# Attention with an expert layer behind it: four more of the 24 attention steps turned by VectorE, and the routing begun half a pair sooner

## Chip, cores and metric

The kernel runs on one core of one Trainium2 chip. The metric is the device time of one execution in microseconds (us); lower is better. Several runs are taken and their median is given.

## What is computed

Two layers, one behind the other, in float32.

```python
# attention: B, H, S, D = 4, 8, 768, 64, in blocks of 64 rows, with a decay lam per head
for each block:
    intra = ((q k^T) * Dmask) v
    out   = intra + (q * lam_pow) kv_state
    kv_state = lam**64 * kv_state + (k * rev_pow)^T v
x = out as (B, S, 512)
# expert layer: 8 experts, 512 -> 1024 -> 512
logits = x @ w_gate; keep = sigmoid(x @ w_local) >= 0.5
e[b, s] = e[b, s-1] if keep[b, s] and s > 0 else argmax(logits[b, s])
out[b, s] = softmax(logits[b, s])[e] * (relu(x[b, s] @ w1[e]) @ w2[e])
```

Of a token's expert nothing is known before its own row of x, and that of every earlier kept token of its sequence, are there.

## The kernel before

**Attention in steps.** A step is 128 rows of one batch; step s (counted from 0, as in the code) is batch s % 4 of chunk s // 4, so there are six chunks of four steps. Steps 6 to 23 run in pairs in one loop (`for s in range(PAIRS, NS, 2)`, with `PAIRS = 6`); "pair 14" below is steps 14 and 15. The order of the instructions on each engine is the order in which the code issues them (`tc.manual_schedule`): nothing overtakes on its engine.

A pair s issues, in this order: DMAs of finished rows (`group_out`) and of weight pieces; `prepare` (POOL scales q and k); `scores(s+1)` and `scores(s+2)` (PE, L217) and `masked` of both (DVE, L225, two instructions a step); `from_state` of both steps (PE, L252, with eight small ACT multiplies that fade the state, L256); what `middles[s]` holds; `mix` of both (PE, L265, and ACT copies of the result to `xc`, L268); what `betweens[s]` holds; `turn(s)`; `update` of both (PE, L282, and DVE adds it to the state `kv`, L285); loads for later steps; what `lasts[s]` holds; `turn(s+1)`.

**The banks.** Scores and state updates write to four banks of PSUM, two pairs of them (`pk`, `ps`) that change roles from pair to pair. The second scores of a pair go to the banks that the state updates of the pair before have just left, so PE waits there for DVE's L285; scores of the step after a masked one wait for DVE's L225 in the same way. Routing results that pass through PSUM use the same banks, or `pl` and `pr`.

**Rows of x.** The attention result stands in `xc` with the features on the partitions; the expert layer gathers tokens by rows from `x_dram`. There are two ways there. `rows_of(s)`: four PE transposes (L293), an ACT copy (L298) and a DMA of one step (L301). `turned_rows(s)`: one DVE transpose (L314), collected over the steps of a chunk, then four DMAs for the chunk (`group_out`, L321). The table `TURNED` names the steps that go the second way and the place at which DVE turns them.

**Routing.** Per chunk: `gates` (PE, L328, ACT copy `lg`, L331), `logits` (PE transposes L336, DVE reduce L337). For chunks 0 to 2 and the fourth chunk apart: `fresh_experts` (L435 to L439), `along_sequences` (PE L447, DVE `stay` L450, DVE scan `run` L456), `experts_of` (PE L463, DVE `hot` L465), `ranks` (PE L474 and L475, DVE scan L483, then L487 to L493, the last two `place`), `masks` (DVE `lane`, L499). From the first three chunks (steps 0 to 11) the tokens of three first tiles are chosen while attention is still running: `first_tiles`, `first_ends`, `tokens_to_first_tiles`, `owners` (L541 to L545), `brought` (L664, L673), `by_slots` (PE L683, DVE `got` L692 to `gidx` L697). Then POOL gathers the tokens (`ahead`, L807), which are transposed (`first_turned`, PE L816, DVE L817), and the first expert tile begins with `hidden` (PE, L838). Behind attention come three such tiles, then eight units that stream the remaining weights, with POOL scattering the results.

Of the kernel before, what the change touches and what calls it, by code (L numbers as in the profile page):

```python
# [23 lines left out]
P = 128  # L24
# [45 lines left out]
def kernel(  # L70
# [289 lines left out]
    def constants_1():  # L360
# [8 lines left out]
        nc.gpsimd.memset(onesb, 1.0)  # L369
        nc.gpsimd.memset(ones8, 1.0)  # L370
# [70 lines left out]
    def along_sequences(i, pr=pr):  # L441
# [8 lines left out]
        nc.vector.tensor_scalar(stay, prow, 0.0, None, ALU.is_equal)  # L450
# [7 lines left out]
    def experts_of(i):  # L458
# [9 lines left out]
    def ranks(i, pr=pr):  # L468
# [23 lines left out]
        nc.vector.tensor_scalar(place[:, 0, lo:hi], rank, P - 1, None, ALU.bitwise_and)  # L492
        nc.vector.tensor_scalar(place[:, 1, lo:hi], rank, -P, None, ALU.bitwise_and)  # L493
# [64 lines left out]
    def first_ends():  # L558

        table, ends, more, tiles = (nows[n] for n in ("table", "ends", "over", "tiles"))  # L560
        nc.vector.tensor_tensor(more, more, tiles.unsqueeze(1).broadcast_to([P, E, E]), ALU.mult)
        nc.vector.tensor_reduce(ends, more, axis=AX.X, op=ALU.add)
        nc.vector.tensor_tensor(tiles, tiles, ends, ALU.add)
        nc.vector.tensor_scalar(ends, ends, float(KA), None, ALU.min)
        nc.vector.tensor_scalar(tiles, tiles, float(KA), None, ALU.min)
        nc.vector.tensor_tensor(taken, tiles, ends, ALU.subtract)
        nc.vector.tensor_tensor_scan(ends, ones8, taken, 0.0, ALU.mult, ALU.add)
        nc.vector.tensor_tensor(table[:, 0], ends, taken, ALU.subtract)
        nc.vector.tensor_copy(table[:, 1], taken)

    def tokens_to_first_tiles():
# [5 lines left out]
        nc.vector.scalar_tensor_tensor(to, late, float(P * AWAY), to, ALU.mult, ALU.add)  # L577
        owners(0, 0, KA, nows["ends"], 0)
# [303 lines left out]
    def number(k, n, engines=None):  # L882
# [14 lines left out]
        8: lambda x: (logits(1), fresh_experts(0)), 10: lambda x: experts_of(0), 12: lambda x: (logits(2), fresh_experts(1)),  # L897
        14: lambda x: experts_of(1), 16: lambda x: (rows_of(14, pl), rows_of(15, pr), first_ends()),
# [16 lines left out]
    with tc.manual_schedule(engines={PE, DVE, SP, POOL, ACTE}):  # L915
# [58 lines left out]
        for s in range(PAIRS, NS, 2):  # L974
# [570 lines left out]
```

## Time and profile before

| | |
|---|---|
| median of 3 runs (lowest to highest) | 403.49 us (403.45 to 404.9) |
| profiled execution: time, and its span | 403.04 us, 401.3 us |
| PE, PEld busy | 391.1 us (97%), 362.8 us (90%) |
| DVE, ACT, POOL busy | 297.7 us (74%), 215.4 us (54%), 184.4 us (46%) |
| granted clock of PE, mean | 0.997 |
| read from HBM, written | 81.55 MB, 12.91 MB |

PE is TensorE's matmuls, PEld its weight loads (they run beside the matmuls of the ones before), DVE VectorE, ACT ScalarE, POOL GpSimd, SP the engine whose queue carries most DMAs. The attention pairs of this page run from about 27 to 91 us of the span; the expert work fills the rest, with PE at nine tenths or more in every slice but the first and the last. A wait is read from a row's bracket: the idle time of its engine before it, and what released it. Where the bracket says "issue", no released semaphore accounts for the idle time.

### The profile page before, as it was taken

How to read it: one execution, taken by the hardware profiler on the slowest of the kernel's cores; microseconds unless marked ns; L12 is line 12 of the kernel's file. 1: busy time of each engine (PE TensorE's matmuls, PEld its weight loads, DVE VectorE, ACT ScalarE, POOL GpSimd, SP SyncE). 2: the span in 40 equal slices, each digit the busy share in tenths (PEclk: the TensorE clock that was granted, in tenths of full speed). 3: DMA queues.
4: the chain of work that ended last, by engine and by line, in shares of the span. 5: the costliest groups of instructions: out<-in, count | busy, mean ns of one | idle time of the engine just before them, and what ended most of it. 6: DMA issues, size and time to landing. Idle time of an engine off the chain costs nothing. (4 is left out here: it accounts for less than half of the span.)

```text
span 401.3 us, 9727 instructions
## 1 busy us (share of the span) xinstructions
PE 391.1 (97%) x3729; PEld 362.8 (90%) x3729; DVE 297.7 (74%) x570; ACT 215.4 (54%) x658; POOL 184.4 (46%) x228
## 2 busy tenths in 40 slices
PE   7999999999999999999999999999999999999994
PEld 6788988878679699999999999999999999999983
DVE  6876989947845889878868768686776868677931
ACT  4236355446715758767557755944854684460310
POOL 5589677330125312174272277157227605701741
PEclk9999999999999999999999999999999999999998
DMA  7999999999999977357346266273545606100101
GB/s 272 417 425 402 416 399 389 340 311 284 390 399 372 406 274 263 96 185 279 118 171 222 70 233 223 97 235 94 206 119 200 265 29 237 51 0 8 45 35 60
DMA packets 37145, 90.67 MB, mean 226 GB/s; under 512 B 3344, under 2 KB 12064, under 8 KB 35424
## 3 DMA queue, kind: packets, MB, share of 16 engines
q1 hardware_dynamic: 31920, 76.57, 52.1%
q0 software_dynamic: 5152, 13.38, 9.5%
q8 instruction: 31, 0.51, 0.5%
q14 instruction: 26, 0.21, 0.2%
q10 hardware_dynamic: 16, 0.00, 0.0%
HBM read 81.55 MB, written 12.91 MB: 235 GB/s over the span
## 5 line engine op out<-in xcount | busy, mean ns | idle before, releaser
L1207 POOL DMA_INDIRECT out_dram<-yq,sidxq x80 | 89.2, 1115 | 103.3 <-DVE yq L1195 69.9
L1152 PE MATMUL ps<-arena,s 128*128 128x148 f32 (+7 forms) x384 | 63.1, 307 | 0.0
L1152 PEld LDWEIGHTS ps<-arena,s 128*128 128x128 f32 x384 | 57.3, 190 | 0.4 <-DVE part L1336 0.3
L807 POOL DMA_INDIRECT xg<-x_dram,gidx x27 | 30.1, 1117 | 52.5 <-DVE w L1123 14.6
L1152 PE MATMUL po<-arena,w 128*128 128x148 f32 (+7 forms) x256 | 41.9, 307 | 0.0
L1152 PE MATMUL ps<-arena,w 128*128 128x148 f32 (+7 forms) x256 | 41.9, 307 | 0.0
L828 ACT COPY arena<-xlast 32x128 f32<-32x128 f32 x128 | 37.8, 295 | 4.8 <-DVE xlast L821 2.1
L1152 PEld LDWEIGHTS ps<-arena,w 128*128 128x128 f32 x256 | 38.3, 190 | 0.5 <-issue 0.5
L1152 PEld LDWEIGHTS po<-arena,w 128*128 128x128 f32 x256 | 38.2, 190 | 0.0
L188 POOL TENSOR_TENSOR qd<-inp,lamq 128x256 f32<-128x256 f32 x40 | 29.5, 759 | 16.7 <-DMA inp<-in_qkv_dram 6.5
L828 ACT COPY arena<-lg 32x128 f32<-32x128 f32 x120 | 35.5, 296 | 2.6
L1190 PE MATMUL pk<-h,w 128*128 128x148 f32 (+6 forms) x224 | 35.1, 310 | 0.0
L1190 PE MATMUL pk<-hsum,s 128*128 128x148 f32 (+6 forms) x224 | 35.1, 310 | 0.0
L1190 PEld LDWEIGHTS pk<-h,w 128*128 128x128 f32 x224 | 33.4, 190 | 0.0
L1190 PEld LDWEIGHTS pk<-hsum,s 128*128 128x128 f32 x224 | 33.4, 190 | 0.0
L256 ACT ACTIVATE kv<-kv,lamq 128x64 f32<-128x64 f32 x64 | 16.4, 335 | 24.0 <-PE po L252 24.0
L1171 ACT COPY arena<-xlast 32x128 f32<-32x128 f32 x88 | 26.9, 305 | 1.9
L194 POOL TENSOR_TENSOR kd<-inp,rev 128x256 f32<-128x256 f32 x40 | 23.8, 615 | 7.9 <-DMA inp<-in_qkv_dram 7.8
L1308 ACT ACTIVATE h<-ps 128x296 f32<-128x296 f32 (+6 forms) x14 | 6.4, 458 | 36.8 <-PE ps L1152 36.8
L225 DVE TENSOR_TENSOR sm<-ps,mask 128x512 f32<-128x512 f32 x30 | 19.2, 682 | 9.1 <-PE ps L217 9.0
L838 PEld LDWEIGHTS ps<-xt,w 128*128 128x128 f32 x192 | 22.1, 192 | 1.9 <-issue 1.0
L838 PE MATMUL ps<-xt,w 128*128 128x128 f32 x192 | 22.7, 276 | 0.0
(333 smaller groups left out, 777.1 us busy)
## 6 DMA issues: line engine op xcount, KB each, us to landing
w<-in_w_dram SPq DMA_DIRECT2D x22, 2048.0 KB, 9.4
inp<-in_qkv_dram SPq DMA_DIRECT2D x13, 1024.0 KB, 11.9
inp<-in_qkv_dram SPq DMA_DIRECT2D x14, 512.0 KB, 9.6
w<-in_w_dram SPq DMA_DIRECT2D x4, 1024.0 KB, 10.2
x_dram<-w SPq DMA_DIRECT2D x12, 256.0 KB, 9.6
inp<-in_qkv_dram SPq DMA_DIRECT2D x4, 768.0 KB, 10.8
x_dram<-xn SPq DMA_DIRECT2D x6, 256.0 KB, 8.4
out_dram<-yq,sidxq POOLq DMA_INDIRECT x80, 3.9
```

The costliest lines, as they stand in the source:

```text
L188: nc.gpsimd.tensor_tensor(qd[:, heads], x[:, 0].rearrange("p (a i) -> p a i", i=P)[:, heads], lamq[:, heads], ALU.mult)
L194: nc.gpsimd.tensor_tensor(kd.rearrange("p (h d) -> p h d", d=DH)[:, heads], x[:, 3].rearrange("p (h d) -> p h d", d=DH)[:, heads], rev[:, ...
L225: nc.vector.tensor_tensor(sm[:, u], ps[u], mask[:, u], ALU.mult)
L256: nc.scalar.mul(kv[:, a], kv[:, a], lamq[:, a, P - 1:P])
L807: nc.gpsimd.indirect_dma_start(out=xg, out_offset=None, in_=x_dram[:n, :], in_offset=bass.IndirectOffsetOnAxis(ap=gidx[i][:, j:j + 1], axi ...
L828: copy((xt(k) if callable(xt) else xt)[QP * j:QP * j + QP, :, at(k):at(k) + QP], blocks[QP * k:QP * k + QP, :, j])
L838: nc.tensor.matmul(ph[:, j], lhsT=w1t[w][:, d, P * f:P * f + P], rhs=xtt[i][:, d], start=(d == 0), stop=(d == DT - 1))
L1152: nc.tensor.matmul(to[:, j], lhsT=a[:, k, P * m:P * m + P], rhs=b[:, k], start=(new and not j and not k), stop=(k == 1), skip_group_check= ...
L1171: nc.scalar.copy(xu[QP * j:QP * j + QP, u % 2::2 - u % 2, :, P + QP // 2 * k:P + QP // 2 * k + QP // 2], blocks[QP * k:QP * k + QP, :, j]. ...
L1190: nc.tensor.matmul(to[:, m], lhsT=a[:, f, P * m:P * m + P], rhs=b[:, f], start=(new and not m and not f), stop=(f == FT // 2 - 1), skip_gr ...
L1207: last = nc.gpsimd.indirect_dma_start(out=out.rearrange("n (j d) -> (n j) d", j=4), out_offset=bass.IndirectOffsetOnAxis(ap=sidxq[:, u, i, ...
L1308: relus(hu[f, i][:, lo:hi, :W], c, ACT.Relu)
```

## The change

- Steps 16 to 19 (the 17th to 20th) are turned by DVE: 16 and 17 in the middle of pair 20, 18 and 19 at `turn(20)`. Their `rows_of` (16 PE transposes, four ACT copies, four DMAs) are gone; four DMAs of the chunk take their place, and the chunk is collected in a tile of the load pool.
- `masked(20)` and `masked(22)` are issued after the middle of their pair (`LATE`).
- `gates`, `ranks`, `along_sequences`, `experts_of`, `logits` and `masks(0)` move half a pair forward.
- The fading of the state is four ACT instructions a pair, over both batches, for eight.
- `stay` is made by ACT for DVE; `place` is one instruction for two; `first_ends` six for nine; `owners` moves from pair 18 to pair 20, behind `gidx`; two blocks of constants move to step 2.

```diff
-TURNED = {**{r: ... for r in range(3 * B)}, 12: 15, 13: 16, 20: 22, 21: 22, 22: 23}
+TURNED = {**{r: ... for r in range(3 * B)}, 12: 15, 13: 15.5, 16: 19.5, 17: 19.5, 18: 20, 19: 20,
+          20: 22, 21: 22, 22: 23}
+LATE = [(20, 18), (22, 20)]
...
+    def fade(s, n=1):
+        b, c = ORDER[s]
+        if c and c + 1 < NC:
+            for a in range(A):
+                kv = kvs[:, b:b + n, a]
+                nc.scalar.mul(kv, kv, lamq[:, a, P - 1:P])
...
-            if k + 1 == NC:
+            if k > 3:
                 xn = load.tile([P, 4, DM], F32, name="inp").rearrange("p n m -> p (n m)")
...
-        nc.vector.tensor_scalar(stay, prow, 0.0, None, ALU.is_equal)
+        nc.scalar.activation(stay, prow, ACT.Relu, bias=1.0, scale=-1.0)
...
-        nc.vector.tensor_scalar(place[:, 0, lo:hi], rank, P - 1, None, ALU.bitwise_and)
-        nc.vector.tensor_scalar(place[:, 1, lo:hi], rank, -P, None, ALU.bitwise_and)
+        nc.vector.tensor_tensor(place[:, :, lo:hi], rank.unsqueeze(1).broadcast_to([P, 2, n]),
+                                bits.unsqueeze(2).broadcast_to([P, 2, n]), ALU.bitwise_and)
...
     middles = {
-        8: lambda x: gates(1, x[0]), 10: lambda x: along_sequences(0, x[1]), 12: lambda x: (ranks(0, x[1]), gates(2, x[0])),
-        14: lambda x: along_sequences(1, x[1]), 16: lambda x: (turn(16), ranks(1, x[1]), gates(3, x[0])),
-        18: lambda x: logits(3, x[0]), 20: lambda x: (by_slots(0, (0, 1), x[0]), gates(4, x[1]), rows_of(18, x[0])), 22: lambda x: logits(4, x[0]),
+        8: lambda x: (logits(1, x[0]), fresh_experts(0)), 10: lambda x: experts_of(0, x[1]),
+        12: lambda x: (logits(2, x[0]), fresh_experts(1)), 14: lambda x: experts_of(1, x[1]),
+        16: lambda x: (turn(15.5), logits(3, x[0])), 18: lambda x: first_ends(),
+        20: lambda x: (by_slots(0, (0, 1), x[0]), first_owners(), turn(19.5)), 22: lambda x: logits(4, x[0]),
     }
     betweens = {
-        8: constants_2, 10: constants_3, 14: lambda: masks(0), 16: first_tiles, 18: lambda: (masks(1), tokens_to_first_tiles()),
+        12: lambda: masks(0), 16: first_tiles, 18: lambda: (masks(1), tokens_to_first_tiles()),
...
     lasts = {
-        8: lambda x: (logits(1), fresh_experts(0)), 10: lambda x: experts_of(0), 12: lambda x: (logits(2), fresh_experts(1)),
-        14: lambda x: experts_of(1), 16: lambda x: (rows_of(14, pl), rows_of(15, pr), first_ends()),
-        18: lambda x: (rows_of(16, pl), rows_of(17, pr), brought(0, (0, 1))), 20: lambda x: rows_of(19, x[1]),
+        6: lambda x: gates(1, pl), 8: lambda x: along_sequences(0, pr), 10: lambda x: (gates(2, pl), ranks(0, pr)),
+        12: lambda x: along_sequences(1, pr), 14: lambda x: (gates(3, pl), ranks(1, pr)),
+        16: lambda x: (rows_of(14, pl), rows_of(15, pr)), 18: lambda x: (gates(4, pl), brought(0, (0, 1))),
...
             for r in (s + 1, s + 2):
-                if r < NS:
+                if r < NS and (r, s) not in LATE:
                     masked(r)
...
+            if (s + 2, s) in LATE:
+                masked(s + 2)
```

The order of DVE's instructions in pair 12, from the scan of `ranks(0)` on. Before (`incl`, `where`, `rank`, `place` belong to `ranks(0)`, `lt` to `mark` to the logits of chunk 2 and `fresh_experts(1)`; the masks of steps 13 and 14 stood ahead of all this):

```order
L483 SCALAR_TENSOR_TENSOR incl_942<-go_127,tot_939 128x72
...
L493 TENSOR_SCALAR place<-rank_947 128x8
L314 STREAM_TRANSPOSE w_1_77<-xc 128x512 x2
L285 TENSOR_TENSOR kv_108<-pk_159,kv_108 128x256
L285 TENSOR_TENSOR kv_109<-pk_520,kv_109 128x256
L337 TENSOR_REDUCE lt<-pl 128x36
...
L439 SCALAR_TENSOR_TENSOR mark_1008<-lt,best_1007 128x4
```

Now:

```order
L491 SCALAR_TENSOR_TENSOR incl_873<-go_124,tot_870 128x72
...
L500 TENSOR_TENSOR place<-rank_878,bits 128x2x8
L225 TENSOR_TENSOR sm<-pk_157,mask 128x512
L225 TENSOR_TENSOR sm<-pk_523,mask 128x512
L225 TENSOR_TENSOR sm<-ps_110,mask 128x512
L225 TENSOR_TENSOR sm<-ps_111,mask 128x512
L341 TENSOR_REDUCE lt<-pk_157 128x36
...
L507 TENSOR_TENSOR lane_973<-countb,place 128x1024
L318 STREAM_TRANSPOSE w_1_77<-xc 128x512 x2
L289 TENSOR_TENSOR kv<-pk_157,kv 128x256
L289 TENSOR_TENSOR kv<-pk_523,kv 128x256
```

Between the scan and the adds to the state of steps 12 and 13, on which the second scores of pair 14 wait, stood the rest of `ranks(0)` and two turns; now also four masks, the logits with `fresh_experts(1)` and the 1024-wide `lane` of `masks(0)` stand there.

The order of DVE in pair 20. Before, from the masks of step 21 on:

```order
L225 TENSOR_TENSOR sm<-pk_520,mask 128x512
L225 TENSOR_TENSOR sm<-ps_113,mask 128x512
L225 TENSOR_TENSOR sm<-ps_114,mask 128x512
L692 COPY got_0_1501<-pk_159 128x6
L696 TENSOR_SCALAR src_1503<-got_0_1501 128x3
L697 TENSOR_TENSOR gidx_131<-src_1503,got_0_1501 128x3
```

Now:

```order
L225 TENSOR_TENSOR sm<-pk_523,mask 128x512
L699 COPY got_0_1451<-pk_157 128x6
L703 TENSOR_SCALAR src_1453<-got_0_1451 128x3
L704 TENSOR_TENSOR gidx_128<-src_1453,got_0_1451 128x3
L549 TENSOR_TENSOR own_1456<-ends_1216,count 1x24
...
L553 TENSOR_SCALAR owner_134<-own_1458 1x3
L318 STREAM_TRANSPOSE inp<-xc 128x512 x2
L225 TENSOR_TENSOR sm<-ps_110,mask 128x512
L225 TENSOR_TENSOR sm<-ps_111,mask 128x512
```

The masks of step 22 stood ahead of `got`; now they stand behind it, behind the three `owner` instructions and behind the turns of steps 16 and 17. The scores of step 23 write to the banks that these masks read.

## Rows read from the trace of the kernel before

**Rows 1.** Windows, pairs 14 to 20: length; PE, PEld, DVE, ACT, POOL busy (instructions).

```profile
54.69:61.32 6.63, 6.32 (x132) 5.81 (x131) 6.35 (x17) 3.29 (x13) 5.20 (x8) 1.00 1.04 402
61.32:69.33 8.01, 8.01 (x147) 6.61 (x147) 7.28 (x20) 4.23 (x16) 5.27 (x9) 1.00 1.05 393
69.33:77.14 7.81, 7.42 (x157) 6.66 (x156) 7.50 (x24) 4.39 (x15) 4.08 (x6) 1.00 1.03 362
77.14:85.07 7.93, 7.60 (x157) 5.74 (x156) 4.21 (x15) 3.28 (x8) 3.64 (x4) 1.00 0.97 309
```

**Rows 2.** Timeline of PEld, blocks of pair 16: start us, us, what it is.

```profile
63.30 0.43 PEld L252 LDWEIGHTS po<-qd,kv 64*64 64x64 f32 x16
...
64.48 0.16 PEld L328 LDWEIGHTS pk<-xc,wgt 128*32 128x32 f32 x8
65.48 0.85 PEld L265 LDWEIGHTS po<-sm,inp 128*64 128x64 f32 x16 [0.84 <-issue]
...
67.17 1.07 PEld L282 LDWEIGHTS pk<-inp,kd 128*64 128x64 f32 x32
68.31 0.42 PEld L293 LDWEIGHTS pl<-ident,xc 128*128 128x128 f32 x4
```

**Rows 3.** Timeline of PEld, pairs 18 and 20: logits, mix, rows of step 19.

```profile
72.70 0.42 PEld L336 LDWEIGHTS ps<-ident,lg 128*128 128x128 f32 x4 [0.63 <-DVE sm L225]
...
81.93 0.85 PEld L265 LDWEIGHTS po<-sm,inp 128*64 128x64 f32 x16 [0.17 <-issue]
...
84.48 0.42 PEld L293 LDWEIGHTS pk<-ident,xc 128*128 128x128 f32 x4 [0.17 <-issue]
```

**Rows 4.** Timeline of PEld and ACT: gates of the last chunk and their copy.

```profile
89.86 0.22 PEld L328 LDWEIGHTS pl<-xc,wgt 128*32 128x32 f32 x8 [0.17 <-issue]
...
91.09 0.59 ACT L331 COPY lg<-pl 128x512 f32<-128x512 f32 x1 [1.22 <-PE pl L328]
```

**Rows 5.** Timeline of DVE, pairs 12 and 14.

```profile
51.82 0.84 DVE L483 TENSOR_TENSOR_SCAN incl<-go,tot 128x72 f32<-128x72 bf16 x1 [1.22 <-POOL qd L188]
...
53.75 1.29 DVE L314 STREAM_TRANSPOSE w<-xc 128x512 f32<-128x512 f32 x2
...
58.10 1.28 DVE L225 TENSOR_TENSOR sm<-pk,mask 128x512 f32<-128x512 f32 x2
...
60.07 1.25 DVE L499 TENSOR_TENSOR lane<-countb,place 128x1024 bf16<-128x1024 bf16 x1
```

**Rows 6.** Timeline of DVE, one multiply of ranks: in pair 16, and behind attention.

```profile
66.71 0.56 DVE L488 TENSOR_TENSOR where<-where,hot 128x32 f32<-128x32 f32 x1
...
102.09 0.26 DVE L488 TENSOR_TENSOR where<-where,hot 128x96 f32<-128x96 f32 x1
```

**Rows 7.** Timeline of DVE, pair 20: the first of three instructions to gidx.

```profile
80.96 0.16 DVE L692 COPY got<-pk 128x6 f32<-128x6 f32 x1
```

**Rows 8.** Timeline of DVE behind attention: scan of a later routing part.

```profile
98.57 1.00 DVE L456 TENSOR_TENSOR_SCAN run<-stay,carry,pr 4x384 bf16<-4x384 bf16 x1 [0.32 <-ACT carry L455]
```

**Rows 9.** Timeline of POOL, the first gather; DMA view: its us to landing.

```profile
81.81 1.21 POOL L807 DMA_INDIRECT xg<-x_dram,gidx  x1 [0.62 <-DVE gidx L697]
...
xg<-x_dram,gidx POOLq DMA_INDIRECT x1, 6.4
```

**Rows 10.** Timeline of PE at first_turned and tile 1, and of the SP queue.

```profile
89.27 0.42 PEld L816 LDWEIGHTS ps<-ident,xg 128*128 128x128 f32 x4 [0.17 <-issue]
...
91.58 2.90 SPq L321 DMA_DIRECT2D x_dram<-inp  x4
95.16 0.42 SPq L778 DMA_DIRECT2D w<-in_w_dram  x1
...
107.30 7.31 PE L838 MATMUL ps<-xt,w 128*128 128x128 f32 x64
```

**Rows 11.** Line views of L907 and, below it, of L778: issue to landing.

```profile
DMA to landing us min/median/max: 7.1/10.2/11.7
...
DMA to landing us min/median/max: 7.9/8.3/11.8
```

More of the change, by code (lines that the diff above doesn't have):

```diff
@@ L42 @@
 HALVES = [9, 13, 18, 22]
-TURNED = {**{r: r + 1 if r < PAIRS else r // 2 * 2 + 2 for r in range(3 * B)}, 12: 15, 13: 16, 20: 22, 21: 22, 22: 23}
+TURNED = {**{r: r + 1 if r < PAIRS else r // 2 * 2 + 2 for r in range(3 * B)}, 12: 15, 13: 15.5, 16: 19.5, 17: 19.5, 18: 20, 19: 20,
+          20: 22, 21: 22, 22: 23}
+LATE = [(20, 18), (22, 20)]
 WARM = 5
@@ L166 @@
     NS = len(ORDER)
-    kvs = []
-    for b in range(B):
-        kvs.append(pows.tile([P, A, DH], F32, name=f"kv{b}"))
+    kvs = pows.tile([P, B, A, DH], F32, name="kv")
     xc = att.tile([P, A, B, P], F32, name="xc", bufs=1)
@@ L247, in from_state @@
         if c:
-            kv, qd = kvs[b], qds.pop(s)
+            kv, qd = kvs[:, b], qds.pop(s)
             for a in range(A):
@@ L253, in from_state @@
                                      start=(a < 2), stop=False, skip_group_check=True)
-            if c + 1 < NC:
-                for a in range(A):
-                    nc.scalar.mul(kv[:, a], kv[:, a], lamq[:, a, P - 1:P])
+    def fade(s, n=1):
[4 more added lines that the diff above has]
+                nc.scalar.mul(kv, kv, lamq[:, a, P - 1:P])
     def mix(s):
@@ L273, in update @@
         if c + 1 < NC:
-            kv, vn = kvs[b], x[:, 2].rearrange("p (a u d) -> p a u d", u=2, d=DH)
+            kv, vn = kvs[:, b], x[:, 2].rearrange("p (a u d) -> p a u d", u=2, d=DH)
             kd = kds.pop(s).rearrange("p (a u d) -> p a u d", u=2, d=DH)
@@ L369, in constants_1 @@
         nc.gpsimd.memset(onesb, 1.0)
+        nc.gpsimd.memset(bits[:, 0:1], P - 1)
+        nc.gpsimd.memset(bits[:, 1:2], -P)
         nc.gpsimd.memset(ones8, 1.0)
@@ L406 @@
     place = route.tile([P, 2, NT], I32, name="place")
+    bits = route.tile([P, 2], I32, name="bits")
     late = route.tile([P, NA], F32, name="late")
-    taken = route.tile([P, E], F32, name="taken")
+    table0 = route.tile([P, 2, E], F32, name="table0")
+    taken = table0[:, 1]
     mx0 = route.tile([P, NA], F32, name="mx0")
@@ L456, in along_sequences, with experts_of @@
         nc.vector.tensor_tensor_scan(run, stay, prow, before, ALU.mult, ALU.add)
-    def experts_of(i):
+    def experts_of(i, pr=pr):
         lo, hi = PARTS[i]
@@ L549, in first_tiles @@
         tiles = multiples(0, NA, counts[1], ALU.is_ge, 1)
-        table = nows["table"] = rt.tile([P, 2, E], F32, name="table0", bufs=1)
+        nows["table"] = table0
         ends = nows["ends"] = rt.tile([P, E], F32, name="ends0", bufs=1)
@@ L558, in first_ends @@
     def first_ends():
-        table, ends, more, tiles = (nows[n] for n in ("table", "ends", "over", "tiles"))
+        ends, more, tiles = (nows[n] for n in ("ends", "over", "tiles"))
         nc.vector.tensor_tensor(more, more, tiles.unsqueeze(1).broadcast_to([P, E, E]), ALU.mult)
         nc.vector.tensor_reduce(ends, more, axis=AX.X, op=ALU.add)
[L563 to L566, printed above, removed]
+        nc.vector.tensor_scalar(ends, ends, -1.0, float(KA), ALU.mult, ALU.add)
+        nc.vector.scalar_tensor_tensor(taken, ends, 0.0, tiles, ALU.max, ALU.min)
         nc.vector.tensor_tensor_scan(ends, ones8, taken, 0.0, ALU.mult, ALU.add)
-        nc.vector.tensor_tensor(table[:, 0], ends, taken, ALU.subtract)
-        nc.vector.tensor_copy(table[:, 1], taken)
+        nc.vector.tensor_tensor(table0[:, 0], ends, taken, ALU.subtract)
     def tokens_to_first_tiles():
@@ L577, in tokens_to_first_tiles, with first_owners @@
         nc.vector.scalar_tensor_tensor(to, late, float(P * AWAY), to, ALU.mult, ALU.add)
+    def first_owners():
         owners(0, 0, KA, nows["ends"], 0)
@@ L949 @@
             from_state(s)
+            fade(s)
             if s == 5:
@@ L970 @@
             turn(s)
+            if s == 2:
+                constants_2()
+                constants_3()
         sides.append((warm, pg.tile([P, A, P], F32, name="pk1")))
@@ L992 @@
                 from_state(r)
+            fade(s, 2)
             free = [t.rearrange("p a i -> p (a i)") for t in sides[(s - PAIRS) // 2 % 2]]
@@ L999 @@
                 betweens[s]()
-            if s != 16:
-                turn(s)
+            turn(s)
             for r in (s, s + 1):
```

## The prediction

> **What bounds the kernel now.** I read the windows of the attention pairs first, then the timeline of PEld (where each block of a pair starts), then DVE's timeline against it, then the SP queue and the gather. In the windows [rows 1] PE is busy in all of pair 16 and idle for 0.31, 0.39 and 0.33 us in pairs 14, 18 and 20, so PE bounds: what shortens or delays its chain shortens or delays the end. But DVE stands close behind, 6.35 of 6.63, 7.28 of 8.01 and 7.50 of 7.81 us busy in pairs 14, 16 and 18; only in pair 20 has it room (4.21 of 7.93). Where PE waits, it waits for DVE: the logits of pair 18 wait 0.63 us for masks [rows 3]. The change takes work from PE and gives DVE four turns; at other places it only changes which DVE instruction stands ahead of which. So the question is where PE will wait for DVE.
>
> Half a percent, 2.0 us, is about what a measurement of this kernel can tell from no change. The sum is made against the profiled execution, 403.04 us, a span of 401.3 and 1.74 around it; it lies 0.45 us under the median of the runs.
>
> **The blocks of PE.** From pair 16 [rows 1, 2]: two scores 1.98 us (61.32 to 63.30), the state's part with the small matmuls of ranks 1.18, gates 1.00, two mixes 1.69, two updates 1.14, rows of two steps 1.02 (68.31 to 69.33). Logits are 0.6, taken like the rows of one step: four transposes each.
>
> **What goes.** The rows of steps 16 to 19: 2 x 1.02 = 2.04 us of PE. Old waits that the new order dissolves or puts elsewhere: in pair 14 at least 0.31 (idle); at most 0.6, the length 6.63 less 1.98 + 1.18 + 1.69 + 1.14. In pair 18, 0.39 to 0.63. In pair 20, 0.33 to 0.86: the two mixes there took 2.55 us (81.93 to 84.48 [rows 3]), not 1.69, with no semaphore named. I take 0.5, 0.6 and 0.8. **Together 3.9 us, bounds 3.1 to 4.2.**
>
> **What comes.** Gates, logits, scores and mixes keep their price wherever they stand. New are the places where PE catches up with DVE; I followed both engines' orders, each from a common point.
>
> *C1, pair 14: scores of step 16 wait for the state of step 13.* Both start with gates(2), now at the end of pair 10. PE: gates 1.00, state's part and ranks 1.18, two scores 1.98, logits 0.6, mixes and updates 2.83, a marks matmul 0.1, first scores 0.99: 8.7. DVE: the copy of the logits ends 1.82 us after the gates start [rows 4], a small ACT copy and handover 0.15, then the old stretch from the scan to the first masks of the next step's pair (51.82 to 58.10 [rows 5], 6.28 us: ranks, two turns, state, logits, fresh experts, one step's masks), plus one more step's masks, 1.2 (start to start; 1.28 for the pair), plus `lane`, 1.2: 10.65. The wait is 1.95. The scan in that stretch takes 0.84; if it halves, as a multiply of the same kind of work takes 0.26 on 96 columns behind attention and 0.56 on 32 in pair 16 [rows 6], the wait is 1.5. I take 1.7, bounds 1.4 to 2.0.
>
> The two multiplies [rows 6] differ in that POOL is busy for 5.27 of 8.01 us in pair 16 [rows 1]. The Trainium skill ("SBUF — State Buffer", Who interferes with whom) says that a VectorE instruction with two inputs in SBUF contends with a GpSimd instruction that reads SBUF, and that one of the two then blocks fully, while forms with one such input outside the two-port modes don't contend; the trace agrees in direction (0.56 against 0.26). By that rule the scan keeps its price, and the new `place`, which has two SBUF inputs where the two old ones had one each, may be held up besides: C1 would be 2.0 and the net below +1.5; by the quick price C1 is 1.5 and the net +1.0.
>
> *C2, pair 16.* From gates(3): DVE has 1.97 to the scan, ranks(1) 1.2 (less than the 1.93 of ranks(0), 51.82 to 53.75, for half the columns), a turn 0.61, the first half of the masks 0.6, handover 0.2, 4.6 in all, against PE's 4.2 to the logits; then 2.7 (masks, a turn, the reduce) against 2.3 to the first update, which waits for that reduce. Two waits of 0.4; I take 0.7, bounds 0.4 to 1.4 (ranks at 1.93).
>
> *C3, into pair 20: scores of step 22 wait for the state of step 19.* In pair 18 DVE loses the logits, `owner` and three of `first_ends`, some 1.4 us of 7.50; PE loses rows and logits and gains gates. They come out nearly even: 0.2, bounds 0 to 0.6.
>
> *C4, pair 20: scores of step 23 wait for the masks of step 22.* From the end of by_slots PE has two mixes, 1.69. DVE: handover 0.2; `got` [rows 7] to `gidx`, three instructions, 0.6; the three `owner` ones as much; two turns 1.2; masks 1.2; handover 0.2: 4.0. The wait is 2.3; if the small ones are shorter, 1.8. I take 2.1. Behind the turns on DVE, nothing earlier is late: the ACT copies to `xc` of steps 20 and 21 wait for those turns inside the same wait.
>
> *C5, tile 0's routing.* The scan `run` already waits 0.32 us for ACT [rows 8], and PE for the scan. The `stay` of 4x384 now runs on ACT ahead of that `carry`: between 0.2 and 0.6 (the copy of 128x512 [rows 4]); 0.4, since it has fewer columns than that copy.
>
> **Together 5.1 us, bounds 3.8 to 6.9. Net +1.2; 404.2 us.** With the bounds not all at one end, 402.7 to 405.9.
>
> At nothing: the four fades (ACT is half idle in every pair, 3.3 to 4.4 us of 6.6 to 8.0); constants at step 2, where DVE waits for loads; the shorter `first_ends`, priced in C3. The rows of steps 16 to 19 reach memory later, but the first gathers read only rows of steps 0 to 11.
>
> **Rivals.**
> *R1, faster: DVE is not late.* If DVE's small instructions run at the quick price and the counts above are too long, PE keeps the 3.9 us. For it: ranks and gates come half a pair sooner, just to uncover them. Against it: C4 has no small-price way out, and the gather is next. It starts after `gidx`, takes 0.3 us to POOL and 6.4 to land [rows 9], at 88.2; PE takes it at 89.27 [rows 10], with 1.1 to spare. `gidx` comes perhaps 0.6 sooner (it follows four masks that DVE can't start before their scores), so PE can win 1.7, less C5: 401.7. Should the gather land in 5 us, 400.3.
>
> *R2, slower: weights late.* On SP's queue the last half load of w2 now stands behind the first DMA of chunk 4, which waits for the turn of step 19, by the chains above about 86.8. Queue order makes the last DMA of the last chunk wait for that load's landing, 7.1 to 11.7 us later [rows 11]: 93.9 to 98.5 instead of 94.48 (91.58 + 2.90), and behind it the w1 of tile 1, issued at 95.16 [rows 10], slips by up to 4 us. It lands 7.9 to 11.8 after issue, and PE wants it at 107.30, so the cover is 0.3 to 4.2; from there it decides. Up to +3.7 over the forecast; I take 2.4: 406.6.
>
> *R3, slower: the costs at their upper bounds.* DVE's small instructions at the contended price (C1 2.0, C2 1.4, C3 0.6, 1.4 more than taken), the mixes in pair 20 still stretched (0.8 not regained) and C4 at 2.3: 2.4 more, 406.6 at most; with half of it 405.4.
>
> That the change doesn't do what it says is no case: the orders show each instruction moved.
>
> **Chances.** Forecast 0.58 (a tail of 0.06 above 405.5), R1 0.18 (0.02 of it within half a percent), R2 0.14, R3 0.10 (0.05 of it slower). Faster 0.16, same 0.59, slower 0.25. The range 401.0 to 406.5 leaves out the quick half of R1 and half of R2.
>
> **What would show it.** Right: PEld's L217 of step 16 waits 1.5 or more for DVE's add to the state; the scores of step 23 wait about 2 for DVE's masks; no L293 for steps 16 to 19; first_turned at 89.7 to 90.7 (89.27 before, plus 0.8, since C5 comes later); `run` waits longer for ACT. Wrong: pairs 14 and 20 without such waits and first_turned before 88.5; first_turned waiting for the gather (R1); a wait for DMA at L838 of tile 1 (R2).

## The result, and the profile after

The change made the kernel slower: 409.81 us median of four runs (408.56 to 410.13) against 403.51, ratio 1.0142 [1.0111, 1.0173]. The forecast was 404.2, the range 401.0 to 406.5, so the result lies 3.3 us above the range's upper end. The sign was that of the forecast's sum, +1.2, but its size was five times that.

The profiled execution took 410.07 us, 7.03 more than the one of before. The page of the kernel after, span and busy time by engine:

```profile
span 408.4 us, 9630 instructions
...
PE 394.3 (97%) x3713; PEld 365.0 (89%) x3713; DVE 300.6 (74%) x565; ACT 209.8 (51%) x629; POOL 185.5 (45%) x230
```

PE is busier than before in spite of the rows it no longer turns. The windows of the kernel after, pairs 14, 16, 18, 20, and pair 22 up to the first `hidden` (columns as in [rows 1]):

```profile
55.52:66.57 11.05, 9.20 (x140) 7.51 (x140) 7.05 (x13) 2.92 (x10) 6.99 (x10) 0.85 1.02 400
66.57:74.66 8.09, 7.75 (x143) 6.74 (x141) 6.53 (x18) 3.69 (x12) 3.96 (x6) 1.00 0.98 346
74.66:81.28 6.62, 6.62 (x154) 5.42 (x153) 5.26 (x11) 3.20 (x10) 2.81 (x4) 1.00 0.94 295
81.28:88.00 6.72, 5.34 (x144) 4.61 (x140) 5.80 (x21) 0.59 (x1) 2.10 (x3) 1.00 0.45 145
88.00:97.43 9.43, 7.78 (x112) 5.70 (x112) 6.91 (x15) 2.54 (x8) 2.20 (x3) 0.82 0.74 187
```

Two things stand out beside [rows 1]. PE's idle time (length less busy) is 1.85, 0.34, 0, 1.38 and 1.65 us, 5.2 in all, where pairs 14 to 20 had 1.03 and pair 22 up to `hidden` none. And in pairs 14 and 22 the granted clock is 0.85 and 0.82. One-microsecond windows of the same kernel, and a block of 16 mixes at either level of the clock, show when and what it costs:

```profile
60.00:61.00 1.00, 1.00 (x21) 1.00 (x24) 1.00 (x3) 0.00 (x0) 0.00 (x0) 0.50 1.10 408
...
91.00:92.00 1.00, 1.00 (x28) 1.00 (x24) 0.92 (x3) 0.00 (x0) 0.00 (x0) 0.50 0.45 172
```

```profile
62.03 1.66 PE L269 MATMUL po<-sm,inp 128*64 128x128 f32 x16
...
93.94 1.09 PE L269 MATMUL po<-sm,inp 128*64 128x128 f32 x16
```

0.50 is the lower of the clock's two levels (1.2 of 2.4 GHz). The engine is busy throughout both windows and yet slower: the 16 mixes that begin at 62.03, most of them inside such a stretch, take 1.66 us, the like 16 at 93.94, behind one, 1.09. The stretches run from 59.8 to 63.2 and from 90.5 to 94.0; by the windows' means they cost PE 0.15 x 11.05 = 1.7 and 0.18 x 9.43 = 1.7 us. The timeline of PE shows what came ahead of each:

```profile
58.53 1.55 PE L217 MATMUL pk<-inp 64*128 64x128 f32 x16 [1.85 <-DVE kv L289]
60.01 1.13 PE L252 MATMUL po<-qd,kv 64*64 64x128 f32 x16
...
83.56 1.12 PE L217 MATMUL ps<-inp 64*64 64x128 f32 x28 [1.32 <-DVE kv L289]
...
89.48 0.43 PE L217 MATMUL ps<-inp 64*64 64x128 f32 x2 [1.54 <-DVE sm L225]
...
106.64 0.22 PE L471 MATMUL pr<-identb,run 4*128 4x4 bf16 x3 [0.47 <-DVE run L464]
```

These are C1 (1.85), C3 (1.32), the first piece of C4 (1.54; the rest of those scores starts at 90.08) and C5 (0.47). The clock falls 1.3 us after PE has come back from C1 (58.53) and 1.0 us after it has from C4 (89.48); it does not fall after C3, the shortest of the three.

**The account.** The first `hidden` starts 6.52 us later (97.43, before 90.91). New idle time 5.2 and half clock 3.4, less the old idle time of 1.03 and the 2.04 of the rows, make 5.5; another 0.83 had gathered ahead of pair 14 (it starts at 55.52, before at 54.69), part of it a wait of PE for `mark`, 0.34 us; the rest wasn't traced. Behind attention the time is nearly that of before: 310.97 us from there to the end, 310.39 before, and C5 is 0.47 of the difference.

### The profile page after: what moved, and what is told of

It is laid out like the page before. It is cut to its first block, busy times and chain, and to the rows that moved or that the text cites. A ratio compares the mean times of both kernels' runs of the same rounds, so it can differ in the third digit from the quotient of the medians.

```text
span 408.4 us, 9630 instructions
## 1 busy us (share of the span) xinstructions
PE 394.3 (97%) x3713; PEld 365.0 (89%) x3713; DVE 300.6 (74%) x565; ACT 209.8 (51%) x629; POOL 185.5 (45%) x230
## 5 line engine op out<-in xcount | busy, mean ns | idle before, releaser
L814 POOL DMA_INDIRECT xg<-x_dram,gidx x27 | 31.4, 1162 | 53.3 <-issue 19.4
L188 POOL TENSOR_TENSOR qd<-inp,lamq 128x256 f32<-128x256 f32 x40 | 28.4, 734 | 23.8 <-PE po L252 11.6
L194 POOL TENSOR_TENSOR kd<-inp,rev 128x256 f32<-128x256 f32 x40 | 24.7, 641 | 6.6 <-DMA inp<-in_qkv_dram 6.5
L260 ACT ACTIVATE kv<-kv,lamq 128x128 f32<-128x128 f32 (+1 forms) x36 | 11.1, 380 | 23.4 <-PE pr L252 15.2
```

What stands on the lines that cost most here:

```text
L188: nc.gpsimd.tensor_tensor(qd[:, heads], x[:, 0].rearrange("p (a i) -> p a i", i=P)[:, heads], lamq[:, heads], ALU.mult)
L194: nc.gpsimd.tensor_tensor(kd.rearrange("p (h d) -> p h d", d=DH)[:, heads], x[:, 3].rearrange("p (h d) -> p h d", d=DH)[:, heads], rev[:, ...
L260: nc.scalar.mul(kv, kv, lamq[:, a, P - 1:P])
L814: nc.gpsimd.indirect_dma_start(out=xg, out_offset=None, in_=x_dram[:n, :], in_offset=bass.IndirectOffsetOnAxis(ap=gidx[i][:, j:j + 1], axi ...
```

## Experiments

The theories: the loss comes from the order of DVE's instructions, or from the turning itself; the half clock is a cost of its own, or is only the shadow of the waits; and something behind attention holds part of the loss. The kernel of before took 403.3 to 403.8 us beside most runs, but 421 beside e1 to e4 and 436 beside e9 to e12, which ran on one and the same other chip. What is longer there lies far behind attention: from unit 0 (137.5 us) to its end e12 takes 295 us, before 263. So ratios are compared, and places inside the first 150 us of the span.

**Turning alone (e1), routing alone (e2).**

```diff
 # e1: before, with
+TURNED = {..., 12: 15, 13: 16, 16: 19.5, 17: 19.5, 18: 20, 19: 20, 20: 22, 21: 22, 22: 23}
+        20: lambda x: (by_slots(0, (0, 1), x[0]), turn(19.5), gates(4, x[1])),
+        18: lambda x: brought(0, (0, 1)),
 # e2: the change, without steps 16 to 19 in TURNED, and with
+        20: lambda x: (by_slots(0, (0, 1), x[0]), first_owners(), gates(4, x[1]), rows_of(18, x[0])),
+        18: lambda x: (rows_of(16, pl), rows_of(17, pr), brought(0, (0, 1))), 20: lambda x: rows_of(19, x[1]),
```

> The kernel before, with only the turning changed: steps 16 and 17 are turned by DVE behind gidx in pair 20, 18 and 19 behind the mixes, and their four rows_of are gone; routing stays where it was. Theory A (the loss comes from PE waiting for DVE at moved routing instructions, and from the clock that falls behind long waits): DVE was idle from 81.5 to 86.0 us there, so the four turns cost nothing, PE saves 2.0 us and is then held by the first gather, which lands at about 88.2: about 402.4 us, no fall of the clock. Theory B (the four turns on DVE, or the rows that reach memory later, cost the time): 406 us or more.

> The changed kernel with the rows of steps 16 to 19 back on PE (rows_of, gates of chunk 4 back in pair 20), all the routing moved as in the change. Theory A: the waits of pair 14 (about 2 us, with the clock falling behind it) and of pair 20 for the state of step 19 (about 1.4) stay, the wait of step 23's scores goes with the turns ahead of it: 407.5 to 409 us. Theory B: near 404 us.

e1: ratio 1.0028 [0.9994, 1.0062], between what its two theories expected (402.4 and 406 us, 0.997 and 1.006), but its first `hidden` starts 1.25 us sooner than before's. The timeline of e1, the four turns on DVE and the first `hidden` on PEld:

```profile
81.42 2.49 DVE L315 STREAM_TRANSPOSE inp<-xc 128x512 f32<-128x512 f32 x4
...
89.66 3.65 PEld L839 LDWEIGHTS ps<-xt,w 128*128 128x128 f32 x32 [0.84 <-DVE got L711]
```

Four turns behind `gidx`, where DVE had room, hold nothing up. Of the 2.04 us of the rows 1.25 reach `hidden`: without them PE waits for the state of step 19 (C3's place), 0.64 us. e2: ratio 1.0115 [1.0054, 1.0176], first `hidden` at 95.94. Its PEld shows C1 and C3 nearly as in the change (after C1 the clock is 0.50 here too, 59 to 62), and no wait for DVE at the scores of step 23, which here find their masks done:

```profile
58.54 2.11 PEld L216 LDWEIGHTS pk<-inp 64*128 64x128 f32 x16 [2.04 <-DVE kv L288]
...
83.62 0.98 PEld L216 LDWEIGHTS ps<-inp 64*64 64x64 f32 x30 [1.33 <-DVE kv L288]
...
90.10 0.75 PEld L216 LDWEIGHTS ps<-inp 64*64 64x64 f32 x32 [0.17 <-issue]
```

So the routing half a pair sooner costs attention 5.0 us by itself; the turning, kept from the masks, gains 1.25. The two don't add up to the change's 6.52, since C4 comes only where both meet, in pair 20. That e1 gains nothing at the end is what the last series is about.

**The half clock (e3, e6), and the change once more (e5).** Matmuls whose results nothing reads fill PE's waits of C1 and C4, 16 (e3) or 8 (e6) ahead of each:

```diff
+BUSY = {16: (None, 8), 23: (1, 8)}        # e3: 16 each
...
+                    for _ in range(n):
+                        nc.tensor.matmul(to[:, :P], lhsT=ident, rhs=ident, ...)
```

> The changed kernel with 16 additional matmuls of 128x128 (about 1.8 us, results not used) on PE ahead of the scores of step 16 and again ahead of those of step 23, that is in the two waits of about 2 us behind which the clock fell. Theory A: the waits for DVE stay as long but PE has work in them, the clock stays at its upper level in pairs 14 and 22, and the time is 408.3 to 408.9 us (a run of the changed kernel at a mean clock of 0.998 took 408.56, those at 0.991 took 410.1). Rival: the clock falls for another reason than the wait: two stretches at half clock stay, and the time is 409.5 to 410.5.

> The changed kernel with eight additional matmuls of 128x128 on PE in each of the two long waits. Sixteen took 3.65 us, twice what was meant, so they outlasted the waits; eight should take 1.8 us and end with them. Theory A (the half clock behind the waits is a cost of its own): no stretch at half clock, the second scores of pair 14 at the same time as in the changed kernel, and the first hidden 2.5 to 3.3 us sooner than in the changed kernel. Rival (a PE at full clock only waits longer at the next place, because DVE sets the pace): first hidden less than 1 us sooner.

> The changed kernel itself, for a reference on the chip of the runs beside it. Both theories: slower than before by 1 to 2 per cent, first_turned's transposes at about 96 us.

e3 (1.0143 [1.0102, 1.0183], `hidden` at 98.36) overshot: 16 took 3.65 us, longer than the waits, and cost at least what the clock gained. In e6 eight, which stand as 16 records, took 1.86 us. Its PEld at C1, and the windows around both places:

```profile
56.59 1.86 PEld L1001 LDWEIGHTS pl<-ident 128*128 128x128 f32 x16
...
58.57 1.23 PEld L218 LDWEIGHTS pk<-inp 64*128 64x128 f32 x16
```

```profile
55.50:66.00 10.50, 10.50 (x172) 9.01 (x173) 7.00 (x14) 3.57 (x13) 6.98 (x10) 1.00 1.03 405
87.00:95.00 8.00, 8.00 (x131) 6.36 (x132) 6.68 (x14) 2.51 (x9) 2.00 (x2) 1.00 0.75 186
```

The scores of step 16 start at 58.57 as in the change (58.53), so the wait of C1 is the same, and the clock stays at 1.00: the next pair starts 1.5 us and `hidden` (94.65) 2.8 us sooner than in the change. That makes the half clock a cost of its own in attention, beside the waits. It isn't there each time: e5, the change unaltered, has one such stretch (58.7 to 62.1) and none behind C4, with `hidden` at 95.89.

How much of this reaches the end is less clear. In the profiled executions e5 is 1.5 us ahead of the change at `hidden` and 0.3 at the end (409.81 us for 410.07), e6 2.8 and 1.9 (408.13). By medians e6 (408.89 us, ratio 1.0142 [1.0109, 1.0175]) is 1.1 us under e5 (410.03, 1.0162 [1.0132, 1.0193]) on the same chip, with intervals that overlap, and its ratio is that of the change's own runs. The mean clocks of those four (0.991, 0.998, 0.991, 0.994 for 410.07, 408.56, 410.13 and 409.56 us) go the same way: from the lowest clock to the highest the time changes by 1.5 us, where 0.007 of the span would be 2.9. So at the end the half clock is worth some 1 to 2 us of the 6.3, and the runs don't set it clear of noise.

**DVE's order put back (e4, e8).** e4 moves `masks(0)`, whose `lane` stood ahead of the adds to the state, back to pair 14; e8 also takes the masks of step 22 to where `by_slots` ends, the turns ahead of it and `owner` behind:

```diff
-        12: lambda: masks(0), 16: first_tiles,
+        14: lambda: masks(0), 16: first_tiles,
 # e8 besides
-        20: lambda x: (by_slots(0, (0, 1), x[0]), first_owners(), turn(19.5)),
+        20: lambda x: (turn(19.5), by_slots(0, (0, 1), x[0]), masked(22), first_owners()),
```

> The changed kernel with masks(0), the 1024-wide lane of 1.7 us, back in pair 14 behind the mixes, so that it stands behind the adds to the state of steps 12 and 13. Theory A: the wait of step 16's scores shrinks from about 2 to about 0.4 us, the clock does not fall in pair 14, and DVE's idle 2.8 us in pair 14 take the lane: 407 to 408 us. Rival (the wait only moves on to pair 16): 409.3 us or more, with a new wait at pair 16's scores or logits.

> The changed kernel with two things put back or aside: lane (masks(0)) in pair 14 as in the run before, and in pair 20 the order turns of steps 16 and 17, by_slots to gidx, masks of step 22, owner, so that only three small instructions and no turns stand between by_slots and the masks on which step 23's scores wait. Theory A: the wait of step 23's scores falls from 2 us to about 0.8, no half clock behind it, and the first hidden comes 2.5 to 3 us sooner than with lane alone put back, at about 92 us. Rival (the late turns of DVE, wherever they stand in pair 20, cost the 2 us): at 94 us or later.

e4's PEld: the wait of C1 is 0.41, and no half clock follows it. C4 and its half clock are still there (the window 88 to 89 has a clock of 0.50).

```profile
56.89 1.29 PEld L217 LDWEIGHTS pk<-inp 64*128 64x128 f32 x16 [0.41 <-DVE kv L289]
```

`hidden` starts at 94.64 in e4 (1.0049 [1.0008, 1.0089]) and 91.90 in e8 (1.0106 [1.0066, 1.0146]), from 95.89 to 97.43 in the change. So the position of one `lane` (1.71 us in the change, beside a POOL multiply; 1.25 before) and, in pair 20, of one step's masks against two turns and `owner` is worth 4.0 to 5.5 us in attention, the half clock included. By ratio e4 is ahead of e8, but the intervals overlap and the chips differ. Yet e8 ends 3.9 us late (407.19 against 403.34) although its `hidden` is only 1.0 late. Its profiled execution, the fastest of its four (405.86), spends 1.8 us more behind `hidden` than before's: here too something behind attention takes a part.

**Behind attention: the weights (e7, e9 to e12).** e7 is e1 with the change's fewer small instructions (`place`, `first_ends`, `owners` moved).

> The kernel before with the turning of steps 16 to 19 behind gidx (as in the run of the turning alone), the one-instruction place, the six-instruction first_ends, and owner behind the turns; routing and lane stay where they were. Theory A: DVE in pairs 16 and 18 sheds about 1.2 us, so that the 0.63 us wait of the logits and the 0.78 us wait of step 22's scores shrink to under 0.3 together, first_turned comes at 86.8 to 87.5 us, and the time is 1.5 to 2.5 us under that of before. Rival (DVE's waits only change places): no faster than the run of the turning alone.

e7 (1.0058 [1.0030, 1.0086]) starts `hidden` 2.15 us sooner than before, at 88.76, and ends 2.4 us later (405.70 against 403.34). Its timelines of the SP queue, of DVE and of PE where tile 1's w1 is issued and where unit 0 begins:

```profile
87.73 8.60 SPq L322 DMA_DIRECT2D x_dram<-inp  x6
...
96.87 0.41 SPq L782 DMA_DIRECT2D w<-in_w_dram  x1
```

```profile
132.08 1.23 DVE L1127 TENSOR_TENSOR s<-w 128x1024 f32<-128x1024 f32 x1 [4.86 <-DMA w<-in_w_dram]
```

```profile
136.58 1.25 PE L1156 MATMUL ps<-arena,w 128*128 128x148 f32 x8 [0.81 <-issue]
...
140.10 1.25 PE L1156 MATMUL ps<-arena,s 128*128 128x148 f32 x8 [2.28 <-DVE arena L1129]
```

The six row DMAs hold the queue 8.60 us (before, four took 2.90 [rows 10]), so tile 1's w1 is issued at 96.87, 8.1 us behind the first `hidden`, not 4.25 (95.16 [rows 10]). From there to unit 0 the DMA engines have no gap (busy share 1.03 from 110 to 130 us; before 1.01 to 1.04 from 100 to 130). Unit 0's own w1 waits for PE to free its buffer and goes out 2.0 us sooner than before, but behind loads that are late. Its issue in e7, and its issue and the DVE instruction that uses it before:

```profile
115.95 0.37 SPq L782 DMA_DIRECT2D w<-in_w_dram  x1
```

```profile
117.96 0.37 SPq L778 DMA_DIRECT2D w<-in_w_dram  x1
...
129.73 1.23 DVE L1123 TENSOR_TENSOR s<-w 128x1024 f32<-128x1024 f32 x1 [0.50 <-DMA w<-in_w_dram]
```

So it is there 16.1 us after its issue (132.08), before 11.8. DVE has waited 4.86 us for it, PE then waits 0.81 and 2.28 with the clock falling behind them (0.90 in 128 to 145). In e5 the same DVE instruction waits 1.93 us, in e6 1.45, in e8 1.81; in the profile of the result it doesn't wait. This is a second bound: attention may end sooner, but unit 0 can't begin before its weights are there. In e5, e6 and e8 it takes back about 1 us of what they won over that profile: their time behind `hidden` is 1.2, 0.8 and 1.3 longer than the 310.97 there, and all of it is lost around unit 0's start. C5, 0.47 us, is in all four.

Putting these loads ahead of the last rows was tried on three kernels: the last three loads at once (e9 on before, e10 on e7, e11 on the change). Beside them stands e12, the small instructions alone on before.

```diff
 # e9, e10, e11: at the start of pair 22, no longer behind the last rows
+                weights_of(0, 1, 1, (1,))
+                nc.sync.dma_start(out=w2t[0], in_=w2_src(e), cond=e != 0, cond_hint=False)
+                weights_of(0, 1, 1, (2,))
```

> The kernel before with one thing moved: on SP's queue the weights of tile 1 (w1, then the conditional w2 of tile 2's predecessor, then w2 of tile 1) go out at the start of pair 22, ahead of the last chunk's row DMAs, not behind them. Theory S (the stream of weights from tile 1 to unit 0 is bound by when it starts: unit 0's w1 landed 34 us after the first of them was issued, and PE has just no reserve there): DVE's first sum of unit 0 no longer waits for DMA (0.50 us before), but PE did not wait there, so the time stays within 0.3 per cent of before. Rival: the weights compete with the last rows and the gather, first_turned waits, 404.5 us or more.

> The run with the turning behind gidx and the smaller routing instructions (first hidden at 88.76 us, 2.1 sooner than before, and yet 0.6 per cent slower), plus the weights of tile 1 ahead of the last rows. Theory S: the wait of PE for unit 0's sums (2.3 and 0.8 us, with half clock behind it) goes, the 2.1 us of attention reach the end: 401 to 401.8 us. Rival (the two chunks of 512-byte rows take the DMA engines' time wherever they stand, so unit 0's weights land no earlier than 131 us): 403.5 us or more.

> The changed kernel plus the weights of tile 1 ahead of the last rows. Theory S: PE's waits at the start of unit 0 (0.5 and 0.4 us) go, the waits of the attention pairs stay: 0.7 to 1.2 us under the changed kernel, about 409 us. Rival: unit 0 is not late in the changed kernel, no difference.

> The kernel before with only the smaller routing instructions (one place, six in first_ends, owner behind gidx); rows of steps 16 to 19 stay on PE. Theory A: the 0.63 us wait in pair 18 shrinks, first hidden 0.5 to 0.9 us sooner; theory S: with only one chunk of 512-byte rows late, the weights of unit 0 land as before, PE waits there for less than 0.5 us: 402.5 to 403.5 us. Rival (the shorter instructions, not the turning, are what delays unit 0): 404.5 or more.

Ratios: e9 1.0025 [0.9978, 1.0073], e10 1.0032 [0.9973, 1.0091], e11 1.0237 [1.0177, 1.0297], e12 1.0004 [0.9964, 1.0044]. The wait at unit 0 is gone in e9, but the last rows come late instead and the routing of the last chunk waits for them, as DVE shows there:

```profile
108.16 0.17 DVE L602 SCALAR_TENSOR_TENSOR left<-taken,incl 128x8 f32<-128x8 f32 x1 [5.91 <-DMA x_dram<-inp]
```

e9 and e10 gain nothing measurable, e11 is the slowest of all. e12 is not to be told from before by its ratio, though its `hidden` comes 1.1 us sooner (89.79).

**Only the first load ahead (e13 to e16); the rows on another queue (e17, e18).** `weights_of(0, 1, 1, (1,))` alone goes to the start of pair 22, in e7 (e13), the change (e14), e8 with the last `stay` back on DVE (e15), and e12 (e16).

> The kernel with the turning behind gidx and the smaller routing instructions (first hidden at 88.8 us, yet slower than before), with the w1 of tile 1 issued in pair 22 ahead of six of the row DMAs, w2 as it was. Theory S (the start of the stream decides): DVE's wait for unit 0's w1 shrinks from 4.9 to under 1.5 us, PE's there from 3.1 to under 0.5, no half clock behind it, and the time is 401 to 402 us where before takes 403.4 (ratio 0.994 to 0.997). Rival (the bytes bind): the wait stays over 3 us, ratio 1.004 or more.

> The changed kernel with the w1 of tile 1 issued in pair 22 ahead of six of the row DMAs. Theory S: PE's 0.9 us of waits at the start of unit 0 go, attention as in the changed kernel: ratio to before 1.012 to 1.0145, where the changed kernel had 1.014 and 1.016. Rival (no effect there): 1.015 or more with the waits still in the profile.

> The changed kernel with four things put back or aside: lane in pair 14, the masks of step 22 ahead of owner and the turns of steps 16 and 17 ahead of by_slots, stay of the last routing part on DVE, and the w1 of tile 1 ahead of the last rows. If the account is complete, what is left of the change costs only the 1.0 us by which the first hidden stood later (91.9 against 90.9): ratio 1.001 to 1.004. If there is a loss not yet named: 1.006 or more.

> The kernel before with the smaller routing instructions alone (first hidden at 89.8 us, rows of steps 16 to 19 on PE) and the w1 of tile 1 ahead of the last rows. Both theories: 1.1 us sooner in attention and no wait at unit 0: ratio 0.996 to 0.999. If the turning pays once the weights are in time, e13 beside it is 0.5 to 1.1 us faster still; if not, it is no faster than this.

e13 1.0082 [1.0058, 1.0106], e14 1.0180 [1.0143, 1.0216], e15 1.0125 [1.0079, 1.0171], e16 0.9970 [0.9953, 0.9986]. With chunk 4 turned by DVE none of the three is better than the kernel it was made from: each ratio is higher, by less than its interval, where 0.994 to 0.997 (e13) and 1.001 to 1.004 (e15) were expected. Without, e16 is faster than before. The SP queue of e13 with the w2 load that stands behind the rows, the wait of PE that ends right after its issue (the profile names no releaser), and the rows of e16, where the same load goes ahead but only the last chunk's four DMAs are left:

```profile
88.47 12.36 SPq L322 DMA_DIRECT2D x_dram<-inp  x6
...
101.19 0.09 SPq L1017 DMA_DIRECT2D w<-in_w_dram  x1
```

```profile
101.35 1.16 PE L852 MATMUL pk<-w,h 128*128 128x512 f32 x2 [3.29 <-issue]
```

```profile
91.31 4.70 SPq L321 DMA_DIRECT2D x_dram<-inp  x4
```

The row DMAs now hold the queue for 12.36 us; 12.0 in e15, with the same 3.3 us of PE; 4.70 in e16. So it is not the place of one load but the rows of chunk 4 together with the last chunk's that block this queue. The last two runs take chunk 4's off it:

```diff
-        nc.sync.dma_start(out=rows[:, P * j:P * j + P]...
+        (nc.gpsimd if k == 4 else nc.sync).dma_start(out=rows[:, P * j:P * j + P]...
```

e17 is e7 with this, e18 is e8 with this and the last `stay` on DVE; chunk 4's four DMAs are issued at the start of pair 22.

> The kernel with the turning behind gidx and the smaller routing instructions (run e7), weights in their old place, and the four row DMAs of chunk 4 issued by POOL behind its second gather. Theory Q (the holding of SP's queue): the w1 of tile 1 goes out at 92 to 93.5 us instead of 96.9, unit 0's w1 lands before 129 us, PE waits there for less than 0.5 us, and the ratio to before is 0.993 to 0.997. Theory D (the time that 512-byte pieces take of the DMA engines): unit 0's w1 lands at 131 us or later, PE waits 1.5 us or more, ratio 1.002 or more.

> The changed kernel with lane in pair 14, the masks of step 22 ahead of owner with the turns ahead of by_slots, stay of the last routing part on DVE, and the row DMAs of chunk 4 on POOL's queue. Theory Q: no wait of PE behind attention, and what is left is the 1.0 us by which the first hidden stands later: ratio 1.001 to 1.004. Theory D: PE waits 0.9 us or more at unit 0, ratio 1.006 or more.

In e17 four row DMAs take 2.70 us of POOL's queue, tile 1's w1 is issued at 93.45, unit 0's is there 12.9 us after its issue (116.39), and DVE's wait shrinks from 4.86 to 1.60 us. POOL, SP and DVE of e17:

```profile
84.25 2.70 POOL L322 DMA_DIRECT2D x_dram<-inp  x4 [0.46 <-DVE inp L315]
```

```profile
93.45 0.50 SPq L782 DMA_DIRECT2D w<-in_w_dram  x1
```

```profile
129.25 1.23 DVE L1129 TENSOR_TENSOR s<-w 128x1024 f32<-128x1024 f32 x1 [1.60 <-DMA w<-in_w_dram]
```

e17: 402.58 us, ratio 0.9969 [0.9956, 0.9981], 0.9 % better than e7 and, with e16 (402.45), one of the two kernels that beat both of the case, by 0.3 %. Theory Q has the ratio and the issue right; its landing before 129 us and its wait of PE under 0.5 us were just missed (129.25; 0.52 at one place). e18, the whole change with three things put back and this queue: 405.45 us, 1.0040 [1.0025, 1.0054], where `hidden` is still 1.0 us late (91.91). Here the wait at unit 0 did not shrink: DVE's is 1.87 us (e8 1.81), PE's 0.34 and 0.52 (e8 0.27 and 0.52), and unit 0's w1 is there 13.1 us after its issue in both. In e18 another DMA of rows holds the SP queue, `xlast`, 4.44 us for 0.99 in e8, and the load behind it goes out 11.4 us behind `hidden`, for 9.4. SP and DVE of e18:

```profile
98.12 4.44 SPq L305 DMA_DIRECT2D x_dram<-xlast  x1
103.30 0.38 SPq L782 DMA_DIRECT2D w<-in_w_dram  x1
```

```profile
132.09 1.23 DVE L1142 TENSOR_TENSOR s<-w 128x1024 f32<-128x1024 f32 x1 [1.87 <-DMA w<-in_w_dram]
```

By ratio e18 is clear of e8 (1.0106), by its profiled execution hardly (405.53 us for 405.86), so what the other queue gave the changed kernel is not settled. Nor is whether a gain is left in the earlier routing.

## Why the prediction was wrong

The step that failed is the sum's pricing of PE's waits: it had C3 too small, let PE come back from C1 and C4 at full speed, and let all that attention gains or loses pass on to the end.

- **What goes**: right. The rows (2.04 us) are gone, pair 18 has no idle time left, and in pair 20 the two mixes are back at 1.7 us. e1 shows the gain alone, with 1.25 us at `hidden`.
- **C1, C2, C4, C5**: right in place and cause, and near in size. Measured 1.85 (taken 1.7), 0.34 (0.7), 2.1 from the end of the mixes at 88.00 to 90.08 (2.1), 0.47 (0.4). Following two engines' orders from a common point carried these to within 0.4 us. For C1 that is luck in part: from gates(2) (47.37 on PEld) to its wait PE took 9.3 us, not 8.7, and DVE's release came after 11.2, not 10.65; `lane` alone took 1.71 for 1.2. Both chains were about half a microsecond too short, and the two errors cancelled.
- **C3**: mis-sized. 1.32 us, taken 0.2 with 0.6 as its bound. The term said that DVE loses 1.4 us of small instructions in pair 18 and that the two engines come out nearly even. A part shows already where only the rows are gone (0.64 us in e1); and the small instructions that are left got dearer. The timeline of DVE in the change, four of `first_ends`, and POOL beside them; then the like in e1, where POOL is not multiplying:

```profile
77.56 0.46 DVE L571 TENSOR_SCALAR ends<-ends 128x8 f32<-128x8 f32 x1
78.05 0.65 DVE L572 SCALAR_TENSOR_TENSOR table<-ends,tiles 128x8 f32<-128x8 f32 x1
78.74 0.67 DVE L573 TENSOR_TENSOR_SCAN ends<-ones,table 128x8 f32<-128x8 f32 x1
79.44 0.65 DVE L574 TENSOR_TENSOR table<-ends,table 128x8 f32<-128x8 f32 x1
```

```profile
77.26 2.81 POOL L188 TENSOR_TENSOR qd<-inp,lamq 128x256 f32<-128x256 f32 x4 [3.91 <-issue]
```

```profile
71.03 0.17 DVE L565 TENSOR_SCALAR ends<-ends 128x8 f32<-128x8 f32 x1
71.31 0.17 DVE L567 TENSOR_TENSOR taken<-tiles,ends 128x8 f32<-128x8 f32 x1
71.51 0.17 DVE L568 TENSOR_TENSOR_SCAN ends<-ones,taken 128x8 f32<-128x8 f32 x1
```

  Four of them take 2.4 us for 0.7, each about as long as one of POOL's four multiplies (2.81 / 4 = 0.70): moving them half a pair put them beside POOL. The Trainium skill ("SBUF — State Buffer", Who interferes with whom) says that a VectorE instruction with two inputs in SBUF contends with a GpSimd instruction that reads SBUF, and that one of the two then blocks fully; the trace agrees for the three with two inputs (0.65 to 0.67 us). The prediction weighed this for the scan of C1 and not for these.
- **The clock**: the largest term that the sum lacked. It priced the waits and let PE come back at full speed. The two waits of some 2 us were each followed by 3.4 us at half the clock, which cost PE 1.7 us each in the profile; e6, without them, starts `hidden` 2.8 us sooner. At the end they are worth less, some 1 to 2 us, and in e5 one of the two didn't come.
- **Behind attention**: taken as passing on whatever attention gave, but for C5. The forecast less C5 puts `hidden` at 91.7 (90.91 and 0.8). e8 starts it at 91.90 and still takes 407.19 us, 405.86 in its fastest execution, 3.0 and 1.7 over the forecast: with attention as forecast, the forecast would still have been too low.
- **Pairs 10 and 12**: 0.83 us, for which there was no term; the first wait that the sum prices is that of pair 14.
- **Rivals.** R1 was wrong. R3's mechanism came true in C3. R2 had the right queue and the wrong place: in the change tile 1's w1 goes out 4.0 us behind `hidden`, before 4.25, and PE doesn't wait for it. What comes late in the variants is unit 0's w1, 35 us on (DVE waits there in e5, not in the profile of the result). That decides in e7. The half load of w2 that R2 put in the way of the rows lands at 98.4 in the change, where the last chunk's row DMAs go out from 98.15, behind DVE's turn: it holds up next to nothing.

The answer on the parts: the turning was sound in attention; the earlier routing lost the time by where its instructions stand on DVE, in waits and in the half clock after two of them. For the turning alone, the row DMAs of chunk 4 on the SP queue took the gain back (e7, e17); for the whole change, what holds unit 0's weights stays in part open (e18).

## What to carry to other kernels

Where an engine stands close behind the one that bounds, ask of each instruction moved not what it costs but which add or mask now stands behind it. Price a new wait with the clock that comes after it, from any row of the trace at the lower level, or give it a range that holds one. And before counting on a stage that ends sooner, follow the chain of loads behind it: in e7 rows that held a DMA queue for 8.60 us undid a gain of 2.15, at a load 35 us on.

## What the runs showed of the hardware

- In the change the granted clock fell to 0.50 for 3.4 us, 1.3 and 1.0 us after PE had resumed from waits of 1.85 and 1.54 us, and not after one of 1.32. In e5, the same kernel, it fell 0.2 us after the first (58.7) and not after the second; with 1.86 us of unused matmuls in the waits (e6) it stayed at 1.00.
- Six DMAs of 512-byte rows held the SP queue 8.60 us in e7, and 12.36 and 12.0 with a weight load put ahead of them (e13, e15); four took 2.90 (before) and 4.70 behind such a load (e16), and four on POOL's queue 2.70 (e17). The profile doesn't name what the queue waits for; that it is the earlier transfers is argued. For it: a row DMA's issue that was held ends at 93.39 in before, 106.10 in e14 and 103.14 in e15, and a load ahead lands at 93.30, 105.98 and 103.22. Against it: in e16 the rows are issued by 96.01, and the load ahead lands at 99.64. In the change the six stand over 6.54 us, but 2.7 of these are a wait for DVE's turn.
- An eight-column DVE instruction took 0.17 us (e1), and 0.46 to 0.67 beside a POOL multiply (the change), 0.46 the one with a single tensor input (L571).
